# Batch 1's attention in a fused attention and MLP kernel: where batch 2's squares, totals and root are made, and how the output matmuls are shared out

## The chip, the cores and the metric

The kernel runs on one core of one Trainium2 chip. The metric is the device time of one execution in microseconds (us), the median of a few runs. The core has five engines, each with a queue of its own that is worked through in order: TensorE (PE in the profile; its weight loads are listed as PEld), VectorE (DVE), ScalarE (ACT), GpSimd (POOL) and SyncE (SP, which here only issues DMAs). They wait for each other by semaphores, which the framework sets from the tiles that instructions read and write. The order on each engine is the order in which the kernel's Python code emits the instructions (`manual_schedule`): nothing is reordered by a scheduler.

## The reference

Eight batches, 12 heads, 448 positions, head size 64. q and k are normalised by the root of their mean square and multiplied by a gain, then attention is taken with v; the heads are laid side by side (768 columns) and go through a two-layer MLP with a tanh GELU (768 to 2048 to 768).

```python
def _attn_ref(q, k, v, g_q, g_k):
    def rmsnorm(x, g):
        return x / np.sqrt(np.mean(x * x, axis=-1, keepdims=True) + 1e-06) * g
    q_n, k_n = rmsnorm(q, g_q), rmsnorm(k, g_k)
    scores = 1.0 / np.sqrt(64) * np.matmul(q_n, k_n.transpose(0, 1, 3, 2))
    attn = softmax(scores)
    return np.matmul(attn, v)

x = attn_out.transpose(0, 2, 1, 3).reshape(8 * 448, 768)
out = gelu_tanh(x @ w_in) @ w_out
```

## The kernel before

**Batches and stages.** The loop at L732 goes over the batches. A batch's 12 heads are three chunks (c = 0, 1, 2) of four heads. For batch b the loop body emits the first MLP matmuls of batch b (`mm1`, L387, and `mm1_pair`, L451, each followed by a GELU on ACT into the tile g), and then the attention of batch b+1 (`attention`, L474). Between the attention's instructions it places the second MLP matmuls of batch b, the output matmuls (`mm2`, L407), so that PE has work while ACT and DVE catch up. Batch 0's attention is emitted by `first_attention` ahead of the loop. "The second attention" is batch 1's, emitted in the loop's first pass (b = 0 in the loop, b = 1 inside `attention`); its PE work starts at 53.47 us, and batch 1's first MLP matmuls follow at 84.76 us.

**One attention.** It has 21 units: for chunk c and key tile t, four score matmuls (L298) into a pair of PSUM banks and one exponential on ACT (L302) into `ex`. Units go out in eight groups (`cuts`): 3, 3, 3, 2, 2, 3, 2, 3. After each group's units a number of output matmuls follows: `first` after the first group, the steps of `shares` (scaled to what is left) after the next six, `last` after the eighth, and `tail` at the end (`upto(quota)`). For batch 1 the quota is 96, which gives 23, 9, 9, 8, 8, 10, 9, 16 and 4; from batch 2 on it is 112. In the fourth and seventh groups the row sums of chunks 0 and 1 are made (`products(..., 0)`, L349, matmuls with a tile of ones), transposed and inverted on DVE (`turned` L358, `recips` L364 and L365, which gives the row `rb`); in the fifth group chunk 0's product with v is made (`products(..., 1)`, L349) and multiplied by `rb` into xT (`quad_x`, L373). Chunks 1 and 2 are finished behind the last group. Before the row sums, DVE may add up some of the `ex` tiles (`key_sums`, L318, L320, L323, L324), so that fewer sums matmuls are needed: `added` (L304) gives how many, (4, 0, 4) for batch 1's chunks, 6 from batch 2 on.

**PSUM.** Units, row sums and products take pairs from three PSUM pairs in turn (`pair`, L68), so a unit waits until the exponential, the transposes or the product that reads the pair three places ahead of it is done. Output matmuls take one of two single banks, 16 matmuls (f = 0 to 15) for each half of an output tile, and the bank is then copied to SBUF (the eviction, L430 on DVE; for part of the last batch L428 on ACT). SP sends a tile off when both halves are copied (L439); batch 0's three tiles have their second halves last.

**The tile g.** One SBUF tile of 16 x 896 bf16 in each partition: for each f, columns 0 to 447 hold the GELU results of an even batch and 448 to 895 those of an odd one. The output matmul of a tile i reads 128 columns of each f as its weights (L407's weight load). In batch 1's attention they are tiles 0 to 2 of batch 0, columns 0 to 383. At the start of the kernel parts of g serve as room for squares (`free`, `sqs`).

**Norms of a coming batch.** q and k of a chunk are loaded by SP (`loads`; `late_loads`, L130, does the same behind a one-element DVE memset, L134, so that the load starts only when DVE gets there). They are squared (`square`: L149 on ACT, L151 on POOL) and summed along the head on DVE (`total`, L156); the root is taken for the three chunks at once, on ACT by a logarithm and an exponential (`rsqrt`, L181 and L188), or for batch 1 on DVE by Newton steps (`rsqrt_newton`, L203). POOL multiplies (`normed`, L238), SP transposes by DMA (`dma_trans`), DVE multiplies kT by the gains (`gain`, L285).

For batch 2 this happens during batch 1's attention: its `side` plan (L745 to L748) says ahead of which group a step is emitted. Chunk 0's loads stand ahead of group 1, together with batch 1's `gain(1, 1)`, which waits for a transposing DMA; chunks 1 and 2 are loaded ahead of group 2, where POOL also gets all six squares (chunks 0, 1, 2, q and k each). The squares use two `sq` buffers in turn, so the third waits for the first total. The totals stand ahead of groups 4 (two), 5, 6 and 7 (two), and the root on ACT behind the last group (`ends`). Then ACT loads the GELU table and POOL, after one wait for the last key sum (`gpsimd_waits`, L622), starts to normalise.

```python
side += [(1, lambda: late_loads(2, 0), lambda: gain(1, 1)),
         (2, lambda: late_loads(2, 1), lambda: late_loads(2, 2))]
for c, slots in ((0, (4, 4)), (1, (5, 6)), (2, (7, 7))):
    for n, slot in zip("qk", slots):
        side += [(2, lambda c=c, n=n: square(2, c, n, nc.gpsimd)),
                 (slot, lambda c=c, n=n: total(2, c, n))]
```

Of the kernel before, what the change touches and what calls it, by code (L numbers as in the profile page):

```python
# [8 lines left out]
F32 = mybir.dt.float32  # L9
# [8 lines left out]
def kernel(  # L18
# [125 lines left out]
    def square(b, c, n, eng, hs=both, ts=slice(0, NT)):  # L144
        if (n, b, c) not in sqs:
            sqs[n, b, c] = sqp.tile([P, 2, NT, D], F32, tag="sq", name="sq")
        sq, raw = sqs[n, b, c][:, hs, ts], raws[n, b, c][:, hs, ts]
        if eng is nc.scalar:
            nc.scalar.activation(sq, raw, AF.Square)  # L149
        else:  # L150
            eng.tensor_mul(sq, raw, raw)  # L151

    def total(b, c, n, hs=both, ts=slice(0, NT)):
        if b not in sss:
            sss[b] = smp.tile([P, NCH, 2, 2, NT], F32, tag="ss", name="ss")
        nc.vector.reduce_sum(  # L156
            sss[b][:, c, "qk".index(n), hs, ts], sqs[n, b, c][:, hs, ts], axis=AX.X
        )
# [44 lines left out]
    def rsqrt_newton(b):  # L203
# [15 lines left out]
        for i, c in enumerate((1, 0, 2)):  # L219
# [5 lines left out]
                op0=ALU.add, op1=ALU.mult,  # L225
            )

    def idle(n, w):

        for _ in range(n):  # L230
            nc.tensor.matmul(w, zeros[:, :128], zeros, start=True, stop=True)
# [71 lines left out]

    def added(b, c):  # L304

        return NT - 1 if b > 1 else (4, 0, 4)[c] if b else 0

    def key_sums(b, c, t):

# [85 lines left out]
        )  # L395

    out_v = out.rearrange("(r t) d -> t r d", t=NT)
    osbs = {}

    def mm2(b, i, half, f):  # L400

        if f == 0:
            osbs["ps"] = ps_m.tile([128, 512], F32, tag="mm", name="o")
            if half == 0:
                osbs[i] = op.tile([128, d_model], F32, tag="osb", name="osb")
        o, osb = osbs["ps"], osbs[i]
        nc.tensor.matmul(  # L407
            o[:, :HD], g[:, f, i * 128:(i + 1) * 128], wout[:, f, half * HD:(half + 1) * HD],
            start=(f == 0), stop=(f == nf - 1),
        )  # L410
        if f + 1 < nf:
            return
        part = osb[:, half * HD:(half + 1) * HD]

        end = b + 1 == B and i + 1 == 2 * S // 128
        if end:
            ends = [(osb, slice(half * HD, (half + 1) * HD), nc.sync)]
            if half == 0:
                nc.scalar.copy(part, o[:, :HD])
            else:  # L420
                n = HD // 2
                fin = op.tile([128, d_model], F32, tag="osb", name="fin")[:, :n]
                nc.scalar.copy(part[:, :n], o[:, :n])
                nc.vector.tensor_copy(fin, o[:, n:HD])
                ends = [(osb, slice(HD, HD + n), nc.scalar),
                        (fin, slice(HD + n, d_model), nc.sync)]
        elif b + 1 == B and half == 0:
            nc.scalar.copy(part, o[:, :HD])  # L428
        else:
            nc.vector.tensor_copy(part, o[:, :HD])  # L430
        if half == 1 or end:
            if not end:
                ends = [(osb, slice(0, d_model), nc.sync)]
            for j in range(2):
                col = i * 128 + j * R
                r = ((b // 2) * 2 + col // S) * R
                for src, cols, eng in ends:
                    own = src[j * R:(j + 1) * R]
                    eng.dma_start(  # L439
                        out_v[col % S // R, r:r + R, cols], own[:, cols] if src is osb else own  # L440
                    )

    def mm1_pair(i, cs=range(HP), b=0, js=range(2)):

        if cs[0] == 0 and js[0] == 0:
            hs1[i] = pair("hh")
        h = hs1[i]
        for j in js:
            f = 2 * i + j
            for c in cs:  # L450
                nc.tensor.matmul(  # L451
                    h[:, j, :S], win[:, c, f * 128:(f + 1) * 128], xT[b][:, c],
                    start=(c == 0), stop=(c == HP - 1),
                )
        if cs[-1] == HP - 1 and js[-1] == 1:
            nc.scalar.activation(  # L456
                g[:, 2 * i:2 * i + 2, (b % 2) * S:(b % 2 + 1) * S], h[:, :, :S],
                AF.Gelu_apprx_tanh
            )
# [11 lines left out]
            for i, half in order for f in range(nf)  # L471
        ]

    def attention(b, m2, quota, side, ends):  # L474


        units = [(c, t) for c in range(NCH) for t in range(NT)]
        cuts = (0, 3, 6, 9, 11, 13, 16, 18, 21)
        groups = [units[i:j] for i, j in zip(cuts, cuts[1:])]
        first, last, tail = 23, 16, 4  # L480
        sums_at, x_at = {3: 0, 6: 1}, {4: 0}
        shares = (0, 12, 24, 35, 45, 58, 69)
        spread = quota - first - last - tail
        given = 0

        def upto(k):
            nonlocal given
            while given < k:
                m2.pop(0)()
                given += 1  # L490

        before = []
        for i, group in enumerate(groups):
            for fn in side.get(i, ()):
                fn()
            for c, t in group:
                unit(b, c, t)
            for c, t in before:
                key_sums(b, c, t)
            if i in x_at:  # L500
                products(b, x_at[i], 1)
                quad_x(b, x_at[i])
            elif i in sums_at:
                products(b, sums_at[i], 0)
                turned()
            if i == 0:
                n = first
            elif i < len(shares):
                n = spread * shares[i] // shares[-1] - spread * shares[i - 1] // shares[-1]
            else:  # L510
                n = last
            end = given + n

            upto(end - n // 2)
            if i in sums_at:
                recips()
            for c, t in group[:1 if i else 0]:
                key_sums(b, c, t)
            upto(end - n // 4)
            for c, t in group[1 if i else 0:-1]:  # L520
                key_sums(b, c, t)
            upto(end)
            before = group[-1:]
        for fn in ends:
            fn()
        nc.scalar.preload_act_table_set(GELU_SET)

        c = NCH - 1
        products(b, c - 1, 1)
        for c, t in before:  # L530
            key_sums(b, c, t)
        quad_x(b, c - 1)
        products(b, c, 0)
        turned()
        products(b, c, 1)
        recips()
        upto(quota)
        mm1_pair(0, early, b)
        quad_x(b, c)
        mm1_pair(1, early, b)  # L540

    def first_attention(side, mid):

# [186 lines left out]

    m2 = []
    for b in range(B):  # L732
        m1, side, ends = [], [], []
        if b == 0:

            m1 = [(0, lambda: total(1, 1, "q"),
                   lambda: total(1, 1, "k"), lambda: total(1, 2, "q"), lambda: total(1, 2, "k"),
                   lambda: rsqrt_newton(1), lambda: normed_both(1, 1, nc.gpsimd)),
                  (4, lambda: transposed(1, 1), lambda: normed_both(1, 0, nc.vector),
                   lambda: normed_both(1, 2, nc.vector)),  # L740
                  (5, lambda: trans(1, 0)),
                  (7, lambda: trans(1, 2))]
            side += [(1, lambda: late_loads(2, 0), lambda: gain(1, 1)),
                     (2, lambda: late_loads(2, 1), lambda: late_loads(2, 2))]
            for c, slots in ((0, (4, 4)), (1, (5, 6)), (2, (7, 7))):  # L745
                for n, slot in zip("qk", slots):
                    side += [(2, lambda c=c, n=n: square(2, c, n, nc.gpsimd)),
                             (slot, lambda c=c, n=n: total(2, c, n))]  # L748
        elif b + 1 < B:

            m1.append((0, lambda: gpsimd_waits(ess[b, NCH - 1][:1, 0, :1])))
            for c in range(NCH):
                m1 += [(0, lambda c=c: normed_both(b + 1, c, nc.gpsimd)),
                       (4 * c + 4, lambda c=c: transposed(b + 1, c))]
            m1 += [(9, lambda: gain(b + 1, 0)), (14, lambda: gain(b + 1, 1))]
# [27 lines left out]
            break  # L783
        nc.scalar.preload_act_table_set(EXP_SET)
        if b + 2 < B:
            ends.append(lambda: rsqrt(b + 2))
            side += [(0 if b else 4, lambda: load_v(b + 2, 0, HP))]
            if b + 3 < B:
                side.append((1, lambda: loads(b + 3, 0)) if b else (5, lambda: late_loads(3, 0)))
        if b == 0:  # L790
# [3 lines left out]
            rounds += [  # L794
                ps_t.tile([128, 2, 512], F32, tag=f"t{i}", name=f"t{i}") for i in range(3)
            ]
        attention(b + 1, m2, 96 if b == 0 else 112, plan(*side), ends)


# [28 lines left out]
```

## Time and profile before

| | |
|---|---|
| median of 3 runs | 412.73 us (412.64 to 412.80) |
| the profiled execution's own time | 413.23 us |
| its span, first to last instruction | 411.4 us |
| mean granted TensorE clock | 0.998 |
| busy: PE, ACT, DVE, POOL | 97%, 67%, 62%, 30% of the span |
| PE's share of the chain that ended last | 88% |

The profile comes from one profiled execution; its times are counted from the span's start. A busy PE is not PE at its peak: matmuls are pipelined and their ends are modelled. The chain that ended last is followed back from the last instruction, at each step to what released it, so an engine that stands in it for a stretch has set the pace there. A wait is put down to the engine that released it, as inferred from semaphore events. A DMA has an issue, on the queue of the engine that starts it, and a landing some us later.

### The profile page before, as it was taken

Reading aid. Unit: us, or ns where it says so; the run is one execution under the profiler, and the core shown is the slowest. Engines: PE = TensorE matmul, PEld = TensorE weight load, DVE = VectorE, ACT = ScalarE, POOL = GpSimd, SP = SyncE. Lnnn points to the kernel's source line nnn. Section 1 sums busy time; section 2 is a strip of 40 time slices with the busy share of each in tenths; the row PEclk is TensorE's granted clock in tenths of the full one; section 3 lists DMA queues with packets and bytes.
Section 4 is the critical chain, followed back from the end, with each engine's and each line's share of the span. In section 5 each row is a group of like instructions: output and inputs, shape, how many; then the busy total and the mean of one; then the engine's idle time right before and its main releaser. Section 6 shows DMA issues by size and latency. Waiting matters only on the chain.

```text
span 411.4 us, 8048 instructions
## 1 busy us (share of the span) xinstructions
PE 399.4 (97%) x3321; PEld 208.2 (51%) x3321; DVE 256.6 (62%) x414; ACT 273.8 (67%) x366; POOL 124.4 (30%) x102
## 2 busy tenths in 40 slices
PE   8789998999999999999999999999999999999995
PEld 3354554455555555555555555555555555555553
DVE  4999637845689357963688366983698504990010
ACT  6995387637975689738877579748878349744300
POOL 6991306492104540082202740063400900000000
PEclk9999999999999999999999999999999999999999
DMA  8999995869712947239922848319823511111033
GB/s 252 288 234 215 200 216 197 194 145 301 136 44 64 238 74 190 65 64 261 183 58 60 207 109 195 76 25 257 118 61 77 112 26 40 44 35 40 0 78 77
DMA packets 65572, 54.06 MB, mean 131 GB/s; under 512 B 37376, under 2 KB 60544, under 8 KB 65536
## 3 DMA queue, kind: packets, MB, share of 16 engines
q1 hardware_dynamic: 53104, 41.43, 39.2%
q0 software_dynamic: 12128, 11.80, 18.2%
q8 instruction: 26, 0.43, 0.4%
q10 hardware_dynamic: 304, 0.33, 0.3%
q14 instruction: 10, 0.08, 0.1%
HBM read 45.61 MB, written 11.01 MB: 138 GB/s over the span
## 4 chain that ended last, share of the span: by engine, by line
PE 88%; ACT 4%; DVE 4%; DMA 1%; POOL 1%; issue 0%; SPq 0%; ACTq 0%
PE o L407 35%; PE h L387 23%; PE t L298 8%; PE t L451 8%; PE t L349 8%; PE hh L451 4%; ACT ex L302 4%; DVE ss L156 2%; DMA rawq<-in_q_dram 1%; POOL g L151 1%; PE o L349 1%; DVE st L358 1%; PE tp L256 1%; DVE rb L365 1%; ACT g L456 0%; PE sc L298 0%
## 5 line engine op out<-in xcount | busy, mean ns | idle before, releaser
L407 PE MATMUL o<-wout,g 128*128 128x384 bf16 x896 | 156.7, 327 | 0.0
L302 ACT ACTIVATE ex<-t,shift 128x896 bf16<-128x896 f32 x147 | 137.6, 1006 | 26.1 <-PE t L298 24.8
L407 PEld LDWEIGHTS <-g 128*128 128x128 bf16 x896 | 82.5, 98 | 68.9 <-issue 19.0
L387 PE MATMUL h<-xT,win 128*128 128x448 bf16 x504 | 96.5, 352 | 0.0
L156 DVE TENSOR_REDUCE ss<-sq 128x14 f32<-128x896 f32 (+3 forms) x43 | 44.2, 1037 | 53.8 <-ACT sq L149 50.9
L387 PEld LDWEIGHTS <-win 128*128 128x128 bf16 x504 | 49.3, 98 | 46.0
L393 ACT ACTIVATE g<-h 128x448 bf16<-128x448 f32 x84 | 45.7, 544 | 28.1 <-PE h L387 23.0
L430 DVE COPY osb<-o 128x384 f32<-128x384 f32 x51 | 27.7, 543 | 52.6 <-PE o L407 51.5
L298 PE MATMUL t<-qT,kT 64*64 64x448 bf16 x588 | 40.0, 359 | 1.8 <-DVE xT L373 1.1
L456 ACT ACTIVATE g<-t 128x896 bf16<-128x896 f32 x14 | 12.1, 914 | 43.5 <-PE t L451 43.5
L622 POOL COPY mark<-es 1x1 bf16<-1x1 bf16 x6 | 1.1, 177 | 129.2 <-DVE es L320 129.2
L451 PEld LDWEIGHTS <-win 128*128 128x128 bf16 x264 | 25.7, 98 | 24.8 <-issue 2.1
L238 POOL TENSOR_TENSOR nrmq<-rawq,rinv 128x896 bf16<-128x896 f32 (+1 forms) x21 | 34.9, 1660 | 10.2 <-DVE o L223 9.7
L451 PE MATMUL t<-xT,win 128*128 128x448 bf16 x168 | 33.5, 352 | 0.0
L151 POOL TENSOR_TENSOR sq<-rawq 128x896 f32<-128x896 f32 x9 | 15.1, 1683 | 57.8 <-DMA rawq<-in_q_dram 32.5
L298 PEld LDWEIGHTS <-kT 64*64 64x64 bf16 x672 | 16.6, 105 | 31.0 <-issue 25.0
L238 POOL TENSOR_TENSOR nrmk<-rawk,rinv 128x896 bf16<-128x896 f32 x19 | 31.9, 1681 | 0.0
L349 PE MATMUL t<-ex,vb 64*64 64x448 bf16 x588 | 31.6, 350 | 0.0
L365 DVE STREAM_TRANSPOSE rb<-rc 128x896 f32<-128x896 f32 x24 | 26.7, 1111 | 0.8
L358 DVE STREAM_TRANSPOSE st<-t 128x448 f32<-128x448 f32 x42 | 24.6, 624 | 2.4 <-ACT ex L302 2.1
L349 PEld LDWEIGHTS <-vb 64*64 64x64 bf16 x672 | 19.5, 107 | 12.8 <-issue 2.9
L323 DVE TENSOR_TENSOR e<-ex 128x896 bf16<-128x896 bf16 x32 | 19.4, 606 | 8.8 <-ACT ex L302 8.5
(90 smaller groups left out, 335.9 us busy)
## 6 DMA issues: line engine op xcount, KB each, us to landing
out_dram<-osb SPq DMA_DIRECT2D x54, 192.0 KB, 2.7
rawq<-in_q_dram SPq DMA_DIRECT2D x23, 448.0 KB, 4.2
rawk<-in_k_dram SPq DMA_DIRECT2D x23, 448.0 KB, 5.3
vb<-in_v_dram POOLq DMA_DIRECT2D x8, 672.0 KB, 6.8
win<-in_moe_w_in_dram POOLq DMA_DIRECT2D x8, 384.0 KB, 13.8
wout<-in_moe_w_out_dram POOLq DMA_DIRECT2D x2, 1536.0 KB, 24.7
qT<-nrmq SPq DMA_TRANSPOSE x19, 5.0
kT<-nrmk SPq DMA_TRANSPOSE x19, 4.5
```

The source lines that it names most:

```text
L156: nc.vector.reduce_sum(sss[b][:, c, "qk".index(n), hs, ts], sqs[n, b, c][:, hs, ts], axis=AX.X)
L238: eng.tensor_mul(nrms[n, b, c][:, ts].rearrange("p t a d -> p a t d"), raws[n, b, c][:, :, ts], root[:, :, ts].to_broadcast([P, 2, m, D]),)
L298: nc.tensor.matmul(sc[r * R:(r + 1) * R, a, :S], kT[rs, c, t, r], qT[b][rs, c, :, r], start=True, stop=True,)
L302: nc.scalar.activation(ex[:, t], sc[:, :, :S], AF.Exp, scale=scale, bias=shift)
L349: nc.tensor.matmul(o[r][a * D:(a + 1) * D], vb[b % 2][rs, 2 * c + a, i] if what else ones[rs], es[i][rs, a], start=(i == 0), stop=(i == n ...
L358: nc.vector.transpose(st[:, r].rearrange("p a b -> p (a b)"), oas[0][r])
L365: nc.vector.transpose(rb.rearrange("p r s -> p (r s)"), rc.to_broadcast([128, 2 * S // 32, 32]))
L387: nc.tensor.matmul(h[:, :S], win[:, c, f * 128:(f + 1) * 128], xT[b][:, c], start=(c == 0), stop=(c == HP - 1),)
L393: nc.scalar.activation(g[:, f, (b % 2) * S:(b % 2 + 1) * S], h[:, :S], AF.Gelu_apprx_tanh)
L407: nc.tensor.matmul(o[:, :HD], g[:, f, i * 128:(i + 1) * 128], wout[:, f, half * HD:(half + 1) * HD], start=(f == 0), stop=(f == nf - 1),)
L430: nc.vector.tensor_copy(part, o[:, :HD])
L451: nc.tensor.matmul(h[:, j, :S], win[:, c, f * 128:(f + 1) * 128], xT[b][:, c], start=(c == 0), stop=(c == HP - 1),)
```

## The change

Five things are changed. All of them act in batch 1's attention or right behind it; the later batches run the same code as before:

- Own shares: the output matmuls between the groups become 18, 12, 13, 8, 8, 12, 8, 14 and 3.
- `added` gives 2 for chunk 1, so DVE adds three `ex` tiles there; the first of these adds is emitted as before behind the unit, the second (of unit 9) is put off from group 3 to group 4, behind chunk 0's product.
- From group 3 on the evictions go to ACT (`by_act`), four of the six.
- Batch 2's squares: chunk 0's stay on POOL in the two `sq` buffers. Chunk 1's stay on POOL and go to the odd half of g (q in f 0 to 6, k in f 7 to 13, the first 128 four-byte words of the half). Chunk 2's are made by ACT behind the table load at the attention's end.
- Batch 2's totals and root: totals of chunks 0 and 1 move from ahead of the groups' products to the end of groups 3 (one) and 4 (three) (`behind`). ACT's root covers chunks 0 and 1 only; chunk 2's totals and a Newton root on DVE (`rsqrt_last`, 14 instructions on 28 elements, with a PSUM pair for what lies between) are emitted ahead of batch 1's later first MLP matmuls, before POOL's normalising.

```diff
--- before.py
+++ after.py
@@ -225,6 +225,23 @@
                 op0=ALU.add, op1=ALU.mult,
             )
 
+    def rsqrt_last(b):
+
+
+        c, flat = slice(NCH - 1, NCH), "p c n a t -> p (c n a t)"
+        own = pair("root")[:, :, :4 * NT]
+        z, t = own[:, 0], own[:, 1]
+        y, ms = rinvs[b][:, c].rearrange(flat), sss[b][:, c].rearrange(flat)
+        nc.vector.tensor_scalar(ms, ms, 1.0 / D, 1e-6, op0=ALU.mult, op1=ALU.add)
+        nc.vector.tensor_scalar(
+            y.bitcast(I32), ms.bitcast(I32), -0.5, float(0x5F3759DF), op0=ALU.mult, op1=ALU.add
+        )
+        for i in range(3):
+            nc.vector.tensor_copy(z, y)
+            nc.vector.tensor_mul(t, z, y)
+            nc.vector.scalar_tensor_tensor(t, t, -0.5, ms, op0=ALU.mult, op1=ALU.mult)
+            nc.vector.scalar_tensor_tensor(y, t, 1.5, y, op0=ALU.add, op1=ALU.mult)
+
     def idle(n, w):
 
         for _ in range(n):
@@ -303,7 +320,7 @@
 
     def added(b, c):
 
-        return NT - 1 if b > 1 else (4, 0, 4)[c] if b else 0
+        return NT - 1 if b > 1 else (4, 2, 4)[c] if b else 0
 
     def key_sums(b, c, t):
 
@@ -395,7 +412,7 @@
         )
 
     out_v = out.rearrange("(r t) d -> t r d", t=NT)
-    osbs = {}
+    osbs, by_act = {}, []
 
     def mm2(b, i, half, f):
 
@@ -424,7 +441,7 @@
                 nc.vector.tensor_copy(fin, o[:, n:HD])
                 ends = [(osb, slice(HD, HD + n), nc.scalar),
                         (fin, slice(HD + n, d_model), nc.sync)]
-        elif b + 1 == B and half == 0:
+        elif b + 1 == B and half == 0 or by_act:
             nc.scalar.copy(part, o[:, :HD])
         else:
             nc.vector.tensor_copy(part, o[:, :HD])
@@ -471,15 +488,15 @@
             for i, half in order for f in range(nf)
         ]
 
-    def attention(b, m2, quota, side, ends):
+    def attention(b, m2, quota, side, behind, ends):
 
 
         units = [(c, t) for c in range(NCH) for t in range(NT)]
         cuts = (0, 3, 6, 9, 11, 13, 16, 18, 21)
         groups = [units[i:j] for i, j in zip(cuts, cuts[1:])]
-        first, last, tail = 23, 16, 4
+        first, last, tail = (23, 16, 4) if b > 1 else (18, 14, 3)
         sums_at, x_at = {3: 0, 6: 1}, {4: 0}
-        shares = (0, 12, 24, 35, 45, 58, 69)
+        shares = (0, 12, 24, 35, 45, 58, 69) if b > 1 else (0, 12, 25, 33, 41, 53, 61)
         spread = quota - first - last - tail
         given = 0
 
@@ -493,6 +510,8 @@
         for i, group in enumerate(groups):
             for fn in side.get(i, ()):
                 fn()
+            if b == 1 and i == 3:
+                by_act.append(b)
             for c, t in group:
                 unit(b, c, t)
             for c, t in before:
@@ -514,17 +533,27 @@
             upto(end - n // 2)
             if i in sums_at:
                 recips()
-            for c, t in group[:1 if i else 0]:
+            soon = group[:1 if i else 0]
+            if (b, i) == (1, 3):
+                put_off, soon = soon, []
+            elif (b, i) == (1, 4):
+                soon = put_off + soon
+            for c, t in soon:
                 key_sums(b, c, t)
             upto(end - n // 4)
             for c, t in group[1 if i else 0:-1]:
                 key_sums(b, c, t)
             upto(end)
             before = group[-1:]
+            for fn in behind.get(i, ()):
+                fn()
         for fn in ends:
             fn()
         nc.scalar.preload_act_table_set(GELU_SET)
 
+        if b == 1:
+            for n in "qk":
+                square(2, NCH - 1, n, nc.scalar)
         c = NCH - 1
         products(b, c - 1, 1)
         for c, t in before:
@@ -538,6 +567,7 @@
         mm1_pair(0, early, b)
         quad_x(b, c)
         mm1_pair(1, early, b)
+        by_act.clear()
 
     def first_attention(side, mid):
 
@@ -730,7 +760,7 @@
 
     m2 = []
     for b in range(B):
-        m1, side, ends = [], [], []
+        m1, side, behind, ends = [], [], [], []
         if b == 0:
 
             m1 = [(0, lambda: total(1, 1, "q"),
@@ -742,14 +772,22 @@
                   (7, lambda: trans(1, 2))]
             side += [(1, lambda: late_loads(2, 0), lambda: gain(1, 1)),
                      (2, lambda: late_loads(2, 1), lambda: late_loads(2, 2))]
-            for c, slots in ((0, (4, 4)), (1, (5, 6)), (2, (7, 7))):
+
+            half = free.bitcast(F32).rearrange("p (f s) -> p f s", f=nf)[:, :, S // 2:]
+            for i, n in enumerate("qk"):
+                sqs[n, 2, 1] = half[:, i * NT:(i + 1) * NT, :2 * D].rearrange(
+                    "p t (a d) -> p a t d", a=2)
+            for c, slots in ((0, (3, 4)), (1, (4, 4))):
                 for n, slot in zip("qk", slots):
-                    side += [(2, lambda c=c, n=n: square(2, c, n, nc.gpsimd)),
-                             (slot, lambda c=c, n=n: total(2, c, n))]
+                    side.append((2, lambda c=c, n=n: square(2, c, n, nc.gpsimd)))
+                    behind.append((slot, lambda c=c, n=n: total(2, c, n)))
         elif b + 1 < B:
 
             m1.append((0, lambda: gpsimd_waits(ess[b, NCH - 1][:1, 0, :1])))
             for c in range(NCH):
+                if b == 1 and c + 1 == NCH:
+                    m1 += [(0, lambda: total(2, 2, "q")), (0, lambda: total(2, 2, "k")),
+                           (0, lambda: rsqrt_last(2))]
                 m1 += [(0, lambda c=c: normed_both(b + 1, c, nc.gpsimd)),
                        (4 * c + 4, lambda c=c: transposed(b + 1, c))]
             m1 += [(9, lambda: gain(b + 1, 0)), (14, lambda: gain(b + 1, 1))]
@@ -783,7 +821,7 @@
             break
         nc.scalar.preload_act_table_set(EXP_SET)
         if b + 2 < B:
-            ends.append(lambda: rsqrt(b + 2))
+            ends.append(lambda: rsqrt(b + 2, slice(0, NCH if b else NCH - 1)))
             side += [(0 if b else 4, lambda: load_v(b + 2, 0, HP))]
             if b + 3 < B:
                 side.append((1, lambda: loads(b + 3, 0)) if b else (5, lambda: late_loads(3, 0)))
@@ -794,7 +832,7 @@
             rounds += [
                 ps_t.tile([128, 2, 512], F32, tag=f"t{i}", name=f"t{i}") for i in range(3)
             ]
-        attention(b + 1, m2, 96 if b == 0 else 112, plan(*side), ends)
+        attention(b + 1, m2, 96 if b == 0 else 112, plan(*side), plan(*behind), ends)
 
 
 # ---- launch: one core; inputs and outputs as the reference has them ----
```

## The prediction

> **What bounds the kernel now.** I read the page first: TensorE (PE) is busy 97% of a span of 411.4 us and carries 88% of the chain that ended last. So only places where PE stands still, or work taken from PE, can pay. I therefore read the chain in order of time. From 102.92 us on it repeats every 47.2 us (102.92, 150.13, 197.34, ...) with PE lines alone. The one attention in which other engines stand in the chain is that of batch 1 (the second of eight), 53.47 to 84.76. The busy time by stretch compares it with batch 2's attention; columns: stretch and length, then busy us (instructions) of PE, PEld, DVE, ACT, POOL, then granted clock, DMA share, GB/s.
>
> ```profile
> 53.47:84.76 31.29, 28.92 (x317) 14.71 (x317) 23.18 (x44) 22.69 (x25) 13.66 (x10) 1.00 0.82 200
> 102.92:131.87 28.95, 28.95 (x294) 15.18 (x294) 23.30 (x40) 23.32 (x26) 3.86 (x5) 1.00 0.37 78
> ```
>
> Batch 2's attention is PE without a gap; batch 1's has gaps. What it would take without them: in batch 2's, the nine runs of output matmuls (L407) take 3.84+2.06+2.06+1.89+1.73+2.22+1.90+2.71+0.76 = 19.17 us for 112, or 0.171 each. Batch 1's has 96 of them, 16 x 0.171 = 2.74 less, and 52 sums matmuls instead of 12, at 0.048 each (28 take 1.35): 40 x 0.048 = 1.92 more. 28.95 - 2.74 + 1.92 = 28.13. It takes 31.29, so 3.16 us are lost. The chain (start, us, what) says to whom:
>
> ```profile
> 58.45 6.41 ACT ex L302 x7
> ...
> 66.45 1.11 DVE rb L365
> 67.56 0.06 DVE osb L430
> 67.62 0.31 issue
> 67.93 2.06 DVE ss L156 x2
> 69.98 1.01 DVE xT L373
> ...
> 77.71 1.96 DVE ss L156 x2
> ```
>
> First seven exponentials in a row pace PE, since 23 output matmuls stand ahead of the fourth unit and too few ahead of the next ones. Then two totals of batch 2's squares (L156) and an eviction stand on DVE between the reciprocal row rb and the product xT that frees a PSUM pair; PE waits 1.14 us for it.
>
> **The change, part by part.** Ends of moved work are given relative to t, the start of batch 1's second matmul stage (84.76 before).
>
> Own shares (18,12,13,8,8,12,8,14,3 output matmuls instead of 23,9,9,8,8,10,9,16,4): no work added; they fill PE while exponentials run. Walking the queues with the row's times, exponential 5 ends at 60.3 and PE needs its buffer at 60.4: the pacing is gone.
>
> Key sums of chunk 1 on DVE (`added` 0 to 2): 8 sums matmuls fewer, 8 x 0.048 = 0.38 off PE; two more adds on DVE (0.62 each, L318 and L320), one before the transposes, one behind xT. DVE has 23.2 us of work in 31; four evictions (0.55 each, L430) go to ACT, whose same copy takes 0.48 (L428). ACT has 22.7 of 31.3 and takes 1.9 more; each copy stands behind exponentials already done. The cover gone, it would cost 0.48 each. Output DMAs on SP wait for the last three: the 96th matmul's copy ends about t+0.8 (t+1.2 before), so the transposes queued behind them on SP start no later.
>
> Totals behind the products: one total (1.08) instead of two between rb and xT: the 1.14 wait goes; xT then ends about 0.3 before PE needs it.
>
> Chunk 2's squares on ACT behind the table load: 2 x 0.95 (the same form in L149), in ACT's idle 6.90 us ahead of L456. Nothing. Chunk 2's root on DVE: 14 instructions of 28 elements. The trace has none with this PSUM operand; bounds 0.19 (28 wide, L223) and 0.28 (84 wide with its gap, L214), I take 0.22, nearest the 28-wide row: 3.1 us (2.7 to 3.9). With two totals (2.1) behind the last xT (t+2.2) it ends at t+7.5; GpSimd's two normalisations (1.69 each) end at t+10.9. SP reached these transposes at t+11.0 and t+12.3 before: hidden, with some 1.5 us to spare, and past that the gain at t+19.9 has some 3 us more. GpSimd's load of v moves from 76.3 to about 69; it lands in 6.4 us, long before use.
>
> So far 28.13 - 0.38 = 27.75 us, 3.54 less than 31.29.
>
> **The step that turns it: chunk 1's squares in g.** Chunk 1's q and k squares (POOL) go to the unused half of g instead of the two sq buffers. GpSimd then no longer waits for totals. But PE reads the other half of g in every output matmul. In the program as built, the weight load of output matmul 34 (f=1 of its tile) carries a wait for the q square, and that of matmul 41 (f=8) for the k square; before, neither waited for GpSimd. The view is strided over f 0 to 6 and 7 to 13, and what is recorded is the whole stretch between its first and last element. So PE, in order, stands at matmul 34 until GpSimd has squared chunk 1, and behind it stand all units, sums and products.
>
> When does PE get there? 53.47 + 0.76 (3 units) + 18/23 of 3.85 + 0.69 + 2.06 (12) + 0.69 + 0.50 (3) = 61.2 us. When is the square done? DVE, then GpSimd, then the landing of that load:
>
> ```profile
> 59.84 0.45 DVE L285 TENSOR_SCALAR kT<-kT,gcols 128x896 bf16<-128x896 bf16 x1 [1.77 <-DMA kT<-nrmk]
> ...
> 61.59 0.63 DVE L320 TENSOR_TENSOR es<-es,ex 128x896 bf16<-128x896 bf16 x1
> 62.13 0.55 DVE L430 COPY osb<-o 128x384 f32<-128x384 f32 x1
> 62.62 0.06 DVE L134 MEMSET rawq<- 1x1 f32 x1
> ```
>
> ```profile
> 62.11 1.68 POOL L151 TENSOR_TENSOR sq<-rawq 128x896 f32<-128x896 f32 x1 [16.42 <-DMA rawq<-in_q_dram]
> 63.75 1.68 POOL L151 TENSOR_TENSOR sq<-rawk 128x896 f32<-128x896 f32 x1
> 69.07 1.68 POOL L151 TENSOR_TENSOR sq<-rawq 128x896 f32<-128x896 f32 x1 [3.65 <-DVE ss L156]
> ```
>
> ```profile
> rawq<-in_q_dram SPq DMA_DIRECT2D x1, 448.0 KB, 3.2
> ```
>
> The last line is chunk 1's q load. It is issued only after a DVE marker (L134), which stands behind the gain that waits for a DMA until 59.84 and three adds. The eviction leaves from ahead of it, so the marker comes at 62.2, the issue at 62.3, the landing at 65.5. Chunk 0's squares end at about 65.1. So the q square runs 65.5 to 67.2, the k square to 68.9. PE stands from 61.2 to 67.25: 6.05 us; then 7 matmuls (1.2 us) and 0.45 more for k.
>
> **The clock.** 6 us is longer than any idle PE has mid-run here. What the clock does then shows at the two ends: the start (PE in order of time, then the last four of these matmuls, min/median/max ns) and the end, after PE's last matmul at 406.98 (columns as above, the clock is the third figure from the right):
>
> ```profile
> 1.17 6.39 PE L231 MATMUL o<-zeros 128*128 128x448 bf16 x18 [1.17 <-DVE zeros L77]
> ```
>
> ```profile
> L231 PE MATMUL o<-zeros x4: 352/397/581, 6.4 to 7.2; 128*128 128x448 bf16 x4
> ```
>
> ```profile
> 409.00:409.50 0.50, 0.00 (x0) 0.00 (x0) 0.00 (x0) 0.00 (x0) 0.00 (x0) 1.00 0.69 154
> 409.50:410.00 0.50, 0.00 (x0) 0.00 (x0) 0.00 (x0) 0.00 (x0) 0.00 (x0) 0.68 0.44 105
> 410.00:410.50 0.50, 0.00 (x0) 0.00 (x0) 0.00 (x0) 0.00 (x0) 0.00 (x0) 0.50 0.00 0
> ```
>
> The clock halves 2.7 us after the last matmul (0.68 in its half microsecond puts the step at 409.68). At the start, matmuls of 448 columns follow each other every 0.375 us instead of 0.189 (24 in 4.54, L451) until about 6.5, that is for 5.3 us. So I expect the clock to halve in the wait and some 5.3 us of PE work afterwards at half rate: 2.65 us lost. It covers the 0.45 us wait for k, as seven matmuls at half rate take 2.2. Bounds: 0 (no halving) and 3.5 (a third longer; the start is one sample). I take 2.65, the only row.
>
> [...]
>
> **The sum.** Batch 1's attention: 27.75 + 6.05 + 2.65 = 36.45 against 31.29: 5.16 more. Everything later repeats at PE's pace, relative to t, unchanged. The profiled execution took 413.23 (span 411.4 and 1.8 around it), 0.50 above the median 412.73; the stage is the same in both, so 412.73 + 5.2 = **417.9 us**.
>
> **Rivals.**
> (1) The clock stays up, because the idle time falls badly in whatever it is counted over: 27.75 + 6.05 + 0.45 = 34.25, 2.96 more: **415.7**. For it: one row only shows the halving; against: 6.05 is over twice the 2.7 us seen. 0.16.
> (2) The load lands later. Landings of q in this stretch reach 4.0 (median) and 5.4: the wait grows by 0.8 to 2.2, **418.7 to 420.1**, or a third stall follows it. For it: four loads queue together; against: its place in the queue is unchanged. 0.12.
> (3) Faster: the wait ends before PE is there and the gaps go, 412.73 - 3.54 = **409.2**. It breaks even if the q square ends 3.5 us after PE arrives, near 64.7, with the clock up. The three squares alone need 5.0 us from the first landing near 61.8, so 66.8. 0.02.
> (4) The clock halves only briefly and the wait is shorter, so that the two sides cancel within a few tenths: 0.01.
> The forecast has 0.69.
>
> The range: low is rival 1 less 0.3 for a landing that leaves GpSimd alone to set the wait, 415.4; high is the forecast with a landing of 4.0 (+0.8) and a third more of half clock (+0.9), 419.6. It leaves out rival 3, rival 4 and the longer half of rival 2. A measurement of this kernel tells about 0.2% (0.8 us) from no change: faster 0.02, same 0.01, slower 0.97.
>
> **What would show it.** In the changed profile: one PE (weight load) idle of about 6 us near 61.2, ended by POOL's square into g; the granted clock at 0.5 for part of 64 to 73; the exponential row no longer in the chain; no gap before 71 caused by xT; batch 1's attention near 36.5 long, the later rounds 47.2. Wrong would be: no such wait (rival 3); full clock after it (rival 1); or a late transpose of batch 2's chunk 2, seen as PE idle after t.

## The result and the profile after

The changed kernel takes 419.87 us, the median of 4 runs (419.05 to 420.77), where the kernel before, beside it on the same chip, takes 412.76 (412.64 to 413.50): a ratio on record of 1.0156 (95% interval 1.0134 to 1.0178). It is slower, by 7.1 us between the medians against the 5.2 forecast; the median lies 1.97 above the forecast and 0.27 above the range. The ratio on record is smaller than the quotient of these two medians (1.0172): it amounts to 6.4 us, which would lie inside the range. So the loss is known to some tenths only, and a second comparison below gives 6.5. The profiled execution took 420.77 us, with a span of 419.0 and a mean clock of 0.990.

First, batch 1's attention by stretch (columns as in the prediction), from its first unit to the next stage's first matmul:

```profile
54.82:91.45 36.63, 29.92 (x309) 14.82 (x309) 21.71 (x40) 25.36 (x30) 10.79 (x8) 0.91 0.76 172
```

It is 36.63 us long instead of 31.29, with 8 matmuls fewer, and PE is idle in 6.7 us of it, at a granted clock of 0.91. PE in order of time shows one long stand, behind the 33rd output matmul (18 + 12 + 3), so at matmul 34:

```profile
62.47 0.66 PE L424 MATMUL o<-wout,g 128*128 128x384 bf16 x3
69.57 3.38 PE L424 MATMUL o<-wout,g 128*128 128x384 bf16 x10 [6.44 <-POOL g L151]
```

The bracket is the idle time ahead of the group and what ended it: 6.44 us, GpSimd's square into g. POOL in order of time says why it ended so late:

```profile
64.17 1.68 POOL L151 TENSOR_TENSOR sq<-rawq 128x896 f32<-128x896 f32 x1 [17.15 <-DMA rawq<-in_q_dram]
65.81 2.06 POOL L151 TENSOR_TENSOR sq<-rawk 128x896 f32<-128x896 f32 x1
67.83 1.67 POOL L151 TENSOR_TENSOR g<-rawq 128x896 f32<-128x896 f32 x1
69.47 1.67 POOL L151 TENSOR_TENSOR g<-rawk 128x896 f32<-128x896 f32 x1
```

The four squares follow each other without a pause. What PE waits for is chunk 0's q load (issued at 59.16, landed 4.88 us later by the chain) and then three squares in a row. The clock, by stretch:

```profile
66.00:67.00 1.00, 0.00 (x0) 0.00 (x0) 0.33 (x1) 0.00 (x0) 1.00 (x1) 0.56 1.04 394
...
72.00:73.00 1.00, 1.00 (x7) 0.27 (x9) 0.00 (x0) 0.00 (x0) 0.00 (x0) 0.52 0.31 19
73.00:74.00 1.00, 1.00 (x21) 0.41 (x21) 0.00 (x0) 0.67 (x1) 0.00 (x0) 1.00 0.73 68
```

It halves in the microsecond from 66 and is whole again at about 73. Finer slices put the steps at 66.13 and 72.96: 6.83 us at half rate, of which PE worked the last 3.39.

Outside the stage three things can add. **The middle**, from the first MLP matmul of batch 1 to the last matmul of the kernel, is 322.23 us in both profiles (84.76 to 406.99, 91.45 to 413.68): nothing is given back or lost there. **The start** of the stage lies 1.35 us later (54.82 for 53.47). It goes back to a landing early in the kernel; the wait for it is in this row of POOL, first before, then after (the row begins 1.98 us later, of which 1.35 are left at the stage):

```profile
5.71 0.57 POOL L632 TENSOR_TENSOR gprod<-grow 64x32 f32<-64x32 f32 x2 [1.71 <-DMA grow<-in_g_k_dram]
7.69 0.56 POOL L662 TENSOR_TENSOR gprod<-grow 64x32 f32<-64x32 f32 x2 [3.68 <-DMA grow<-in_g_k_dram]
```

**The end**, from the last matmul to the end of the span, is 5.3 us instead of 4.4. So for the two profiled executions: 5.34 of stage, 1.35 of start, 0.9 of end, together 7.6, which is 419.0 less 411.4.

### The profile page after: what moved, and what is told of

Same layout as the page of the kernel before. It is cut to its first block, busy times and chain, and to the rows that moved or that the text cites. A ratio compares the mean times of both kernels' runs of the same rounds, so it can differ in the third digit from the quotient of the medians.

```text
span 419.0 us, 8051 instructions
## 1 busy us (share of the span) xinstructions
PE 399.5 (95%) x3313; PEld 207.9 (50%) x3313; DVE 260.3 (62%) x426; ACT 276.9 (66%) x372; POOL 120.9 (29%) x100
## 4 chain that ended last, share of the span: by engine, by line
PE 89%; ACT 4%; DMA 2%; POOL 2%; DVE 1%; issue 1%; POOLq 0%; ACTq 0%
PE o L424 35%; PE h L404 23%; PE t L366 8%; PE t L315 8%; PE t L468 8%; PE hh L468 4%; ACT ex L319 3%; DMA grow<-in_g_k_dram 1%; DMA rawq<-in_q_dram 1%; PE tp L273 1%; PE o L366 1%; POOL sq L151 1%; PE sc L315 1%; DVE ss L156 0%; ACT g L473 0%
## 5 line engine op out<-in xcount | busy, mean ns | idle before, releaser
L424 PE MATMUL o<-wout,g 128*128 128x384 bf16 x896 | 158.5, 329 | 6.4 <-POOL g L151 6.4
L156 DVE TENSOR_REDUCE ss<-sq 128x14 f32<-128x896 f32 (+3 forms) x41 | 42.2, 1036 | 48.6 <-ACT sq L149 45.4
L447 DVE COPY osb<-o 128x384 f32<-128x384 f32 x47 | 25.6, 544 | 49.7 <-PE o L424 48.6
L151 POOL TENSOR_TENSOR sq<-rawq 128x896 f32<-128x896 f32 x7 | 11.8, 1681 | 50.2 <-DMA rawq<-in_q_dram 32.0
```

Of the source, the lines that this page charges most:

```text
L156: nc.vector.reduce_sum(sss[b][:, c, "qk".index(n), hs, ts], sqs[n, b, c][:, hs, ts], axis=AX.X)
L424: nc.tensor.matmul(o[:, :HD], g[:, f, i * 128:(i + 1) * 128], wout[:, f, half * HD:(half + 1) * HD], start=(f == 0), stop=(f == nf - 1),)
```

## The experiments

My theory: all of the loss is the wait at matmul 34 and the half clock behind it, and the wait exists only because one strided write to g is guarded as a whole stretch; the other four parts are a gain. The rivals: other parts of the change lose time too; and the clock counts for more or less than worked out. In the table the stage runs from the first unit to the next stage's first matmul in PE's list, which ends 0.16 us ahead of the chain's count (31.13 for 31.29); all gaps are PE's idle times in it.

| run | median us (runs), ratio to before | stage from, us | gaps and half clock |
|---|---|---|---|
| before | 412.76 (4) | 53.47, 31.13 | 0.70 ACT ex, 1.14 DVE xT, 0.53 DVE es |
| after | 419.87 (4), 1.0156 | 54.82, 36.46 | 0.27 DVE kT, 6.44 POOL g; half for 6.83 |
| seven_pieces | 410.42 (6), 0.9915 | 54.10, 27.94 | none |
| squares_in_sq | 411.17 (10), 0.9937 | 54.20, 29.03 | 0.24 DVE kT, 0.62 DVE st |
| zeros_in_wait | 417.72 (9), 1.0097 | 52.87, 34.48 | 0.20 and 0.33 POOL g; full clock |
| only_g | 421.17 (4), 1.0171 | 52.92, 39.31 | 0.36 ACT ex, 6.22 POOL g, 0.80 DVE xT, 0.53 DVE es; half for 10.24 |
| old_shares | 411.17 (1) | 53.21, 29.18 | ACT ex, 0.24 and 0.24 |
| dve_evictions | 410.65 (1) | 53.21, 28.55 | none of 0.2 or more; three rows of units 0.2 to 0.3 longer |
| totals_ahead | 411.52 (1) | 53.74, 28.97 | 0.35 DVE kT, 0.61 DVE xT |
| zeros_18 | 421.63 (1) | 55.80, 36.67 | 0.32 DVE kT, 3.17 POOL g; half for 3.41 |
| changed_again | 419.94 (4), 1.0159 | 53.46, 36.75 | 0.24 DVE kT, 6.58 POOL g; half for 6.83 |
| before_again | 414.04 (1) | 54.24, 31.13 | 0.65 ACT ex, 1.14 DVE xT, 0.53 DVE es |

The intervals: seven_pieces 0.9882 to 0.9947, squares_in_sq 0.9914 to 0.9960, zeros_in_wait 1.0072 to 1.0123, only_g 1.0113 to 1.0229, changed_again 1.0124 to 1.0194. The kernel before stood at 413.49 (20 runs) beside the first four of them, and 413.47 (6 runs) beside changed_again; the runs with (1) are single executions.

### seven_pieces: the change without the wait

```diff
-                    side.append((2, lambda c=c, n=n: square(2, c, n, nc.gpsimd)))
+                    if c == 0:
+                        side.append((2, lambda c=c, n=n: square(2, c, n, nc.gpsimd)))
+                    else:
+                        for t in range(NT):
+                            side.append((2, lambda c=c, n=n, t=t: square(
+                                2, c, n, nc.gpsimd, ts=slice(t, t + 1))))
```

> The changed kernel, but chunk 1's q and k squares go to the same places in g as seven writes each (one for each f) instead of one strided write. The result is the same. Theory (the wait comes from the range recorded for the strided write, from its first to its last element): each write now covers only its own piece of the odd half, so no output matmul waits for GpSimd, the clock stays at 1.00 and batch 1's attention takes about 27.8 us: 409.2 us in all, up to 409.6 as fourteen small squares take a little longer than two large ones. Rival A (writing into the tile that PE reads costs by itself, by port or bank): still above 412.8. Rival B (the moved work is late, the wait only hides it): PE idle elsewhere and more than 411. The start and the end of the profiled run of the changed kernel were 1.35 and 0.9 us longer than before; if they belong to the change, the time is near 411.4, if they vary from run to run, 409.2.

Each of chunk 1's squares is written in seven pieces, each of which lies within one f of the odd half. In the program as built, output matmuls 34 and 41 then carry no wait for GpSimd. The result is 410.42 us, 3.1 below the kernel before beside it, where 3.5 was expected; it lies above the 409.2 to 409.6 named, as the kernel before stood 0.8 higher too in this comparison (413.49). The stage by stretch:

```profile
54.10:82.20 28.10, 28.10 (x309) 14.61 (x309) 21.14 (x40) 25.36 (x30) 12.90 (x20) 1.00 0.89 223
```

The same 309 matmuls as in the change, PE busy in 28.10 of 28.10 us, clock 1.00. The price is on POOL, which in order of time has

```profile
66.50 2.54 POOL L151 TENSOR_TENSOR g<-rawq 128x128 f32<-128x128 f32 x7
69.00 2.92 POOL L151 TENSOR_TENSOR g<-rawk 128x128 f32<-128x128 f32 x7
```

2.54 and 2.92 us instead of 1.67 each, and nobody waits for it. This settles the main question: the same places in g, the same work, and only the guard on the write makes the difference between 0.9915 and 1.0156. All the rest of the change together is a gain.

### squares_in_sq: the change without g

```diff
-            for i, n in enumerate("qk"):
-                sqs[n, 2, 1] = half[:, i * NT:(i + 1) * NT, :2 * D].rearrange(
-                    "p t (a d) -> p a t d", a=2)
```

> The changed kernel, but chunk 1's squares use the two sq buffers again and not g; all other parts stay. The result is the same. Theory: no wait of PE for GpSimd. GpSimd must wait for chunk 0's totals instead (about 67.7 and 70.4), so chunk 1's squares end near 69.4 and 72.1 and its totals on DVE end 0.8 us later than with room in g; the next transposes start that much later and PE may wait some tenths at the eighth group: 409.2 to 410.0. Rival B (the other parts lose time by themselves): above 412.8. If the room in g was worth its price without the wait, this is slower than the run with seven pieces by 0.5 us or more; if not, equal within 0.3.

Chunk 1's squares use the two sq buffers again, so they wait for chunk 0's totals. 411.17 us, stage 29.03: 1.1 longer than in seven_pieces. The chain shows it (the lines between are left out):

```profile
70.64 1.52 issue
...
72.19 1.69 POOL sq L151
...
73.91 1.09 DVE ss L156
...
75.47 1.19 DVE st L375 x2
...
76.69 0.38 PE t L315 x4
```

The k square starts only at 72.19, its total on DVE has to wait for it, and the transposes of the sums (st), which free a PSUM pair, stand behind that total; PE waits 0.62 us. Of the 1.1 us, 0.24 is the wait for kT, which comes and goes between the runs; the medians differ by 0.75. So room in g is worth about 0.8 us here, if it comes without the wait; as the intervals of the two ratios overlap, that size rests mainly on the two profiles. The time, 411.17, is above the 409.2 to 410.0 expected.

### zeros_in_wait: PE kept busy through the wait

```diff
             osbs["ps"] = ps_m.tile([128, 512], F32, tag="mm", name="o")
+            if (b, i, half) == (0, 2, 0):
+                idle(30, osbs["ps"][:, :S])
```

> The changed kernel with 30 more matmuls of zeros (448 columns) ahead of output matmul 33, into the bank that this one then starts; they keep PE busy for 5.7 us of its wait of 6.4. The result is the same. Theory (the wait costs its length, and half clock afterwards costs 2.65 more, of which the wait for the k square takes 0.45 back): clock 1.00 throughout, PE goes on at the same moment, and batch 1's attention is 2.2 us shorter: 419.9 - 2.2 = 417.7. Rival (the slow stretch after the wait has another cause, such as GpSimd's writes or the loads that run then): unchanged at 419.9, or 5.7 us longer if the wait isn't on GpSimd at all.

Thirty matmuls with a tile of zeros stand ahead of the 33rd output matmul of the change; they fill the wait and are no part of the result. The wait shrinks to two short gaps, the clock stays at 1.00, and the stage is 34.48 instead of 36.46:

```profile
60.53 5.84 PE L248 MATMUL o<-zeros 128*128 128x448 bf16 x30
...
66.73 1.31 PE L426 MATMUL o<-wout,g 128*128 128x384 bf16 x7 [0.20 <-POOL g L151]
68.37 0.66 PE L426 MATMUL o<-wout,g 128*128 128x384 bf16 x3 [0.33 <-POOL g L151]
```

The last gap is the k square at matmul 41, which the half clock covers in the change. What the half clock costs follows from the two stages, which differ by 1.98: the zeros and the gap behind them take 6.04 (5.84 + 0.20) where the change stands 6.71 (6.44 + 0.27), which is 0.67 of it, and the k gap is 0.33 the other way. 1.98 - 0.67 + 0.33 = 1.64. The time, 417.72, is the 417.7 expected, but by luck: I had PE go on at the same moment and 2.65 for the half clock; the wait was 0.67 shorter, and the half clock was worth 1.0 less.

### only_g: the kernel before with chunk 1's squares in g

```diff
+            half = free.bitcast(F32).rearrange("p (f s) -> p f s", f=nf)[:, :, S // 2:]
+            for i, n in enumerate("qk"):
+                sqs[n, 2, 1] = half[:, i * NT:(i + 1) * NT, :2 * D].rearrange(
+                    "p t (a d) -> p a t d", a=2)
```

> The kernel before with one edit: chunk 1's q and k squares go to the odd half of g by one strided write each, as in the change. The result is the same. Theory: the wait alone. Output matmul 34 is reached at 61.8 and the q square ends near 67.6, so PE waits 5.8 us, then 2.65 us are lost to half clock; of the 3.2 us of gaps of before only some 0.3 go: 412.8 + 8.2 = 421.0, range 419.5 to 421.5. That is slower than the changed kernel by what its other parts are worth less what they no longer find to save. Rival (the wait is harmless, the other parts of the change are what costs): at most 414.

Half of one of the five parts alone (where chunk 1's squares go): 421.17 us, the stage 39.31, 8.18 longer than before and 2.85 longer than with all five. PE stands at the same matmul, and the clock now stays at half longer:

```profile
67.62 2.74 PE L407 MATMUL o<-wout,g 128*128 128x384 bf16 x8 [6.22 <-POOL g L151]
```

```profile
62.00:63.00 1.00, 0.00 (x0) 0.00 (x0) 0.40 (x5) 1.00 (x2) 1.00 (x1) 0.91 0.03 11
63.00:64.00 1.00, 0.00 (x0) 0.00 (x0) 0.00 (x0) 0.39 (x1) 1.00 (x2) 0.50 0.43 66
...
73.00:74.00 1.00, 1.00 (x7) 0.47 (x5) 0.96 (x3) 0.00 (x0) 0.00 (x0) 0.97 0.00 0
```

The third figure from the right falls at 62.8, only 1.4 us after PE's last matmul (ended 61.41), and is back at 73.06: 10.24 us. PE worked the last 5.44 of them at half rate, so 2.7 us are lost instead of the change's 1.7. Here the square of chunk 1 did wait 0.84 us for its own load, which in the change it did not.

### old_shares, dve_evictions, totals_ahead: what the other parts bring

Each takes one part back out of seven_pieces.

```diff
-        first, last, tail = (23, 16, 4) if b > 1 else (18, 14, 3)
+        first, last, tail = 23, 16, 4
...
-        shares = (0, 12, 24, 35, 45, 58, 69) if b > 1 else (0, 12, 25, 33, 41, 53, 61)
+        shares = (0, 12, 24, 35, 45, 58, 69)
```

> The kernel with seven pieces, but with the output matmuls shared out as before (23, 9, 9, 8, 8, 10, 9, 16, 4). The result is the same. Read from batch 1's attention, first unit to first matmul of the next stage: 27.94 us with the new shares. Theory (the old shares let exponentials pace PE): the two gaps of before behind exponentials come back, 0.46 and 0.24: 28.6 (28.4 to 28.9). Rival (with DVE relieved the shares no longer matter): 27.9 to 28.1.

The stage is 29.18, 1.24 longer, where 28.4 to 28.9 was expected: two gaps came back as named, with 0.48 together instead of 0.70, and two rows of units are some 0.2 longer each. The exponentials pace PE again, as this line of the chain shows:

```profile
58.18 5.51 ACT ex L319 x6
```

```diff
-                by_act.append(b)
+                pass
```

> The kernel with seven pieces, but all six evictions of batch 1's attention on DVE. The result is the same. Theory: one copy (0.5) stands again between rb and xT; xT had 0.25 us to spare, so PE waits 0.25 there and about as much at the last key sum: 28.2 to 28.6. Rival (DVE has room enough): 27.9 to 28.1.

28.55, 0.61 longer, within the range expected. With the evictions back on DVE, the chain runs over DVE alone from 64.15 to 75.18; this is where xT comes later, though PE's list has no single wait of 0.2 or more for it:

```profile
66.84 0.06 DVE osb L447
...
67.20 1.07 DVE ss L156
68.27 0.99 DVE xT L390
```

```diff
-            for c, slots in ((0, (3, 4)), (1, (4, 4))):
+            for c, slots in ((0, (4, 4)), (1, (5, 6))):
...
-                    behind.append((slot, lambda c=c, n=n: total(2, c, n)))
+                    side.append((slot, lambda c=c, n=n: total(2, c, n)))
```

> The kernel with seven pieces, but the totals of chunks 0 and 1 ahead of groups 4, 4, 5 and 6 as before and not behind 3 and 4. The result is the same. Theory: a second total (1.0) stands between rb and xT, which had 0.25 us to spare: PE waits 0.75 us there, 28.7 (28.5 to 29.1). Rival (the order of the totals is without effect once the evictions are gone from DVE): 27.9 to 28.1.

28.97, 1.03 longer, within the range expected; 0.61 of it is the wait for xT that the old place of the totals brings; the other gap, 0.35 for kT, waits for a DMA to land and comes and goes between the runs (the table has it in four others, and not in seven_pieces). These three are single executions beside one run of the kernel before (414.11), so their sizes are good to a few tenths.

### zeros_18: only half of the wait filled

```diff
+            if (b, i, half) == (0, 2, 0):
+                idle(18, osbs["ps"][:, :S])
```

> The changed kernel with 18 matmuls of zeros (3.4 us) in the wait instead of 30, so that PE stands still for about 3 us. The result is the same. In the changed kernel the clock halved 3.0 us after PE's last matmul, with one write of squares alone in g 1.4 us after it; both times it stayed halved for a multiple of 3.41 us (6.8 and 10.2). Theory (it is judged at fixed steps of 3.41 us whose place against the wait varies, by how much PE did within one): either no halving, and batch 1's attention takes 34.5 us as with 30, or a halving that lasts 6.8 us at least, and 35.5 to 37.2. Rival (idle time alone counts, from 3.0 us on): no halving, 34.5, whatever the place.

The question was whether idle time alone decides the halving. PE stands 3.17 us, and the clock falls all the same, though only after PE is back:

```profile
70.73 3.11 PE L426 MATMUL o<-wout,g 128*128 128x384 bf16 x10 [3.17 <-POOL g L151]
```

```profile
70.00:71.00 1.00, 0.27 (x2) 0.21 (x3) 0.00 (x0) 0.00 (x0) 1.00 (x2) 1.00 0.92 326
71.00:72.00 1.00, 1.00 (x5) 0.44 (x4) 0.00 (x0) 0.00 (x0) 1.00 (x1) 0.52 0.60 228
...
74.00:75.00 1.00, 1.00 (x20) 0.40 (x12) 0.00 (x0) 0.59 (x1) 0.00 (x0) 0.77 0.77 56
```

1.00 until 71.04, then half until 74.46, while PE works from 70.73. A theory in which the clock falls a fixed time into an idle stretch and rises as soon as PE works doesn't give this; my theory of fixed steps, an estimate from the 6.83 and 10.24 us of after and only_g, leaves room for it, but what makes the clock fall was not shown. That it would be half for 6.8 us or more, if at all, was my miss: it was 3.41. The stage, 36.67, is in the range expected.

### changed_again and before_again: which differences repeat

Both kernels unedited, to see whether the later start and the longer end belong to the change.

> The changed kernel unedited, a second time, to see what of its 7.1 us stays. Theory (batch 1's attention adds 5.3 us, and the start and the end of an execution vary by themselves): against the kernel before on the same chip 5.3 to 6.3 us, and batch 1's attention again between 36.0 and 37.5 us from its first unit, depending on how the steps of the clock fall. Rival (the change lengthens the start or the end as well): 7 us or more again, and its first unit of batch 1 above 54.5 us again.

> The kernel before unedited, for a second profile of its start. Theory: batch 1's attention takes 31.1 us again, and its first unit stands anywhere between 52.8 and 55.8, as it did over the runs so far, set by when the row of k's gains lands. Rival (the place of the first unit is a property of the program): 53.5 within 0.1.

Against the kernel before at 413.47, changed_again's 419.94 is 6.5 us more, just above the 5.3 to 6.3 of my theory. Its half clock lasts from 65.23 to 72.05, 6.83 us again, and PE works the last 3.73 of them. Its stage starts at 53.46, so the 1.35 us of later start don't belong to the change: over all runs it begins between 52.87 and 55.80, in the unedited kernel before at 53.47 and 54.24. The longer end does repeat: 5.2 us after the last matmul, where before, before_again and six of the experiments have 4.4 to 4.5. The two kernels with zeros have 5.4 and 4.9 too.

## Why the prediction was right or wrong

**Direction and mechanism: right.** The wait stands at matmul 34, is ended by GpSimd's q square, and is followed by half clock. seven_pieces takes the wait alone away and the sign turns.

**The gapless stage (27.75): right to 0.35.** Without gaps it is 28.10 by the same count. The gains of the other parts are real: against the kernel before 3.19 us of stage, forecast 3.54.

**The wait (6.05): 6.44, right in size, one cause misnamed.** I had PE set free by the landing of chunk 1's q load (65.5) and one square. In the change that square starts the moment the square ahead of it ends; the landing that counts is chunk 0's, 4.88 us after its issue, and then three squares. The size is partly luck: counted from the first unit, PE came to matmul 34 0.58 later than worked out (0.27 of it is the wait for kT) and was set free 0.97 later, and only the difference, 0.39, shows. One of the squares took 2.06 us instead of 1.68, beside this add on DVE, which otherwise takes 0.62:

```profile
64.58 1.76 DVE L335 TENSOR_TENSOR es<-ex 128x896 bf16<-128x896 bf16 x1 [0.20 <-ACT ex L319]
```

The add begins inside the q square (64.17 to 65.85) and ends 0.5 us behind it, and the k square, begun at 65.81, is longer by 0.38. Why the two take longer beside each other was not shown.

**The half clock (2.65): mis-sized, 1.7 measured.** This is the term of the sum that failed most. I took the 5.3 us of half rate at the kernel's start for the length that PE works at half; here it worked 3.39 us, in changed_again 3.73, in only_g 5.44. That row was no fixed price: the same 18 matmuls of zeros take 6.39 us in the profile before and 5.29 in the profile after, and in zeros_in_wait, which starts as after does, the last of them begins at 6.6 us instead of 6.1; and the profile's clock column reads 1.00 there, before and after. The halved stretches in batch 1's attention are 6.83 (twice), 10.24 and 3.41 us, that is 2, 3 and 1 times 3.41. So what was lost varied between the runs, from a half of 3.39 to a half of 5.44 us. Nor did a long idle stretch stand ahead of every fall: only_g's came 1.4 us after a matmul. How much work keeps the clock up was not measured.

**The stage in all: 36.63 against 36.45.** The terms miss by +0.35, +0.39 and -0.95, and a wait of 0.27 us for kT, which I hadn't, and 0.1 of rest come on top. The sum fits better than its terms, by luck.

**Everything later unchanged: right for PE, wrong for the end.** The root's 14 instructions take 95.95 to 99.06, the 3.1 us forecast; no transpose comes late, and the middle is equal to the last hundredth. But the span ends 0.7 to 0.9 us later behind the last matmul. This term was missing from the sum, which put everything behind the stage at nothing; without it the first median too would lie inside the range: the stage's 5.3 and 5.6 and the end's 0.9 and 0.7 make 6.2 and 6.4 in the two profiles of the change, against 7.1 and 6.5 between the medians; the rest is within the spread of the starts.

**What stays open: the longer end.** In the four runs that have it the last output DMA lands in 2.2 to 2.4 us instead of 1.9, and a packet of an instruction queue (q14) falls in the last 4 us. But squares_in_sq has such a packet there too, and its end is 4.4. Which of the change's instructions brings it, if any, was not shown.

**The rivals.** Full clock (1) is out, as the clock did fall. The time of a late load (2), 418.7 to 420.1, holds the median, but not for its reason: the load that came late was chunk 0's, and what it cost is within the 0.39. Faster (3) is what seven_pieces shows once the wait is gone: 410.42, or 3.1 us less than before, where 3.54 was worked out. Of the versions run it has the lowest median.

## What to carry to other kernels

When a buffer is lent to a second use while the first still reads another part of it, look at which stretch the framework guards: a strided write may be guarded from its first to its last element, and then an engine waits that shares no byte with it. Writing the same places in pieces that are each contiguous where it counts (14 small squares for 2, 2 us more on an idle engine) took away 8.5 us on the bound one. And price a wait of PE of several us with the half clock behind it: it lasted 3.41, 6.83 and 10.24 us here, and half of the part that PE worked through was lost, 1.7 to 2.7 us.

## What the runs showed of the hardware

- The granted clock stayed halved for 6.83 us in the change and in changed_again, 10.24 in only_g and 3.41 in zeros_18: 2, 3 and 1 times 3.41. It fell 3.0 us after the last matmul in the change, 3.5 in changed_again, 1.4 in only_g, and 0.3 us after PE was back from a stand of 3.17 us in zeros_18.
- A bf16 add on DVE (0.62 us alone) took 1.76 us beside a square on POOL, and the next square 2.06 instead of 1.68.
- The first unit of batch 1 begins up to 2.9 us apart (52.87 to 55.80) from run to run. The row of k's gains lands early or late in the kernel (POOL waits 1.7 to 3.7 us for it), which explains most of it, but not all: from that row to the first unit it is 47.1 to 48.4 us. A single profile's span is not good to better than that.
